# A written order of steps in a cross-covariance attention and MLP kernel: the whole order replaced

## The chip, the cores and the metric

One Trainium2 chip, one of its cores. The metric is the device time of one execution in microseconds (us); lower is better. The kernel before takes 698.52 us (median of 3 runs, 698.0 to 699.55).

## The reference

Inputs are q, k and v of shape (4, 6080, 256), w_in (256, 2048) and w_out (2048, 256), all float32; tau is 1.

```python
qn = q / (np.linalg.norm(q, axis=1, keepdims=True) + 1e-06)
kn = k / (np.linalg.norm(k, axis=1, keepdims=True) + 1e-06)
s = kn.transpose(0, 2, 1) @ qn / tau          # 256 x 256 for each batch
a = softmax(s)                                # along the last axis
x = (v @ a).reshape(24320, 256)
h = x @ w_in
g = 0.5 * h * (1.0 + np.tanh(c * (h + 0.044715 * h * h * h)))
out = g @ w_out
```

## The kernel before

**Algebra.** v @ a @ w_in is computed as v @ aw with aw = a @ w_in, so each batch first needs q^T k (tile G), the sums of squares of q and k, the scores, and then aw (256 x 2048, bf16). The 24320 rows are cut into 48 blocks n, 12 for each batch, of 512 rows (448 in the last block of a batch). A block's work is h = aw^T v^T (2048 x rows), gelu, and w_out^T g. Most of both products is done with seven products of half size in place of eight (the Strassen-Winograd scheme), which needs sums and copies on DVE and ACT around the matmuls.

**The steps.** After a fixed opening (first batch's G and squares, scores, the first quarter of aw), everything is written out by hand as a list of strings, `ORDER`, one string for each block. A step is a name and an offset in blocks: `M3A-2` in block 5's string is step M3A of block 3. `step(what, n)` (L934) turns it into instructions; each engine runs its own instructions in exactly this order, and waits for others through semaphores. The steps:

- `g0`..`g7`: pair p of h done directly (`mm1`, L511, matmul L521, four of 512 columns), into one of two bank pairs "h" and "b" in PSUM; `G0`..`G7`: its gelu on ACT (L531).
- `w0`, `w1`, `w2` with `m1`..`m7`: a set of two pairs done with seven products (`small`, L576, matmul L604, two of 256 columns each); `cq`, `y5` (ACT, L620, L623), `ap`, `ax` (DVE, L625, L628) are copies and sums in between, `Gq`, `Gr`, `Gx` (ACT, L630, L635, L638) the gelus. `cq` has to be through before `m6` and `m2`, `ap` before `m3`, `ax` before `m4`.
- `vs`: sums of v^T for the sets on DVE (L558 to L561); `SW0`..`SW2`: sums of aw (L547 to L550).
- `T1a`, `T2`, `T3`, `T4`: sums of g on DVE (L696 to L711); `M1A`..`M7B`: halves of the seven products with w_out (`product`, L716, matmul L736, four of 256 columns); `y5`, `cq` (ACT, L759, L794), `c11`, `ap`, `ax`, `c12`, `c21`, `c22` (DVE, L765, L774, L798): the combination and the 32 x 32 turning of the result. Four turned pieces start the four stores of a block on SP (L835). `D..`: direct products for the last block (L748), `sA`, `sB` its stores (L823).
- `aw2`..`aw7` (L454) and `ac2`..`ac7` (L465, L467): parts of aw and their scaling; `pA..`, `pF..`, `pS..`, `pNA`: sums and casts of w_out; `vtp`, `vtc`, `vtq`, `vtr`: v of blocks 1 and 2 turned on PE and copied by DVE.
- `row0`..`row5` (`gram_row`, L253), `qsq`, `ksq` (L192, L194), `f1`..`f3`, `sp`, `sa`, `pow`, `kf`, ... : the next batch's G, squares, norms and scores.
- `lq`, `lk` (`load_one`, L98, POOL): a chunk of q or k of the next batch, cast to bf16 on the way; `lv` (L152, POOL): a block of v cast to bf16 into DRAM; `lt` (`load_vt`, L162, SP): that block read back transposed. `lq`, `lk` and `lv` also wait until the last matmul of `mm1` or `small` named ahead of them has run (`GATE`), so their place in the order sets their earliest time.

POOL does little but start loads; SP starts the transposing loads and the stores, in the order of the list. w_in comes in five pieces, columns 0 to 256, to 512, to 1024, to 1536 and to 2048, started in the opening (L905); `aw2` and `aw3` need the third piece, `aw4` and `aw5` the fourth, `aw6` and `aw7` the fifth.

Of the kernel before, what the change touches and what calls it, by code (L numbers as in the profile page):

```python
# [18 lines left out]
def kernel(  # L19
# [1004 lines left out]
    w2Gx row1-1 w1m6 w1ap vs+1 M2B-1 M6B-1 M6A-1 w1m7 qsq row0 M2A-1""",
    """g0 ksq w1m2-1 w1m3-1 w1ax-1 w1m4-1 w1Gr-1 c11-2 ap-2 T4-2 w1Gq-1 w2m4-1 M3A-2 lq+2 M3B-2
    sp-2 T1a-1 sa-2 M7A-2 M7B-2 row3 G0 lq+1 w2Gr-1 ksq-1 w0m5 w0m1 w0cq w0y5 row4 c12-2 g3 G3
    w1Gx-1 w0m6 ax-2 M4B-2 w1m1 M4A-2 vs+1 w1m5 w0ap w0m7 c21-2 w0ax T3-1 w0m2 w0m3 M1B-1 lk+2
    w1y5 row3-2 w0m4 w1cq w1m6 M1A-1 M5A-1 M5B-1 w1ap w1m2 w1m3 T2-1 w0Gq w0Gx w1m7 row2 lk+1
    w0Gr y5-1 cq-1 qsq M2A-1 M6A-1 M6B-1 M2B-1 w1Gq f1-1 w1ax w1m4 w2m1 w1Gr w2m5 f2-1 row0-2""",
    """w0m5 c11-2 w0m1 ap-2 M7B-2 T4-2 w2y5-1 w2cq-1 c22-3 M7A-2 ax-2 w2m6-1 w2ap-1 w0cq row1-1  # L1030
    row0-1 w0m6 w0y5 M4A-2 w0ap M4B-2 w2m7-1 w2m3-1 w2m2-1 M3B-2 w0m2 M3A-2 lk+6 w0m7 T1a-1
    w1Gx-1 w2ax-1 qsq+1 w2Gq-1 c12-2 c21-2 w2Gx-1 w2m4-1 w2Gr-1 g0 G0 M1B-1 f3-2 lt+2 w0m3 w0Gq
    sp-2 w0ax M1A-1 vs+1 sa-2 w0m4 w0Gr g3 M5B-1 G3 M5A-1 w2m5 row1+1 y5-1 cq-1 T3-1 lv+3 lt+3
    c22-2 row5-1 w1m1 w1m5 T2-1 w2m1 T4-1 M6A-1 M6B-1 w0Gx w1cq f1-1 w1y5 w1m6 w1ap M2A-1 M2B-1
    c11-1 ap-1 row5 row0+1 lv+7 w2y5 w2cq row0 w2m6 w2ap qsq w1m7 ksq+1 w1m3 w1m2 w1Gq M7A-1
    w1ax w1Gx M7B-1 M3B-1 w2m7 M3A-1 T1a row2+1 w1m4 w2m3 w1Gr w2m2""",
    """w0m5 row5 ax-2 M4B-2 f2-2 f3-2 w2ax-1 sp-2 sa-2 w2Gq-1 M4A-2 row2-1 w0m1 w0y5 g3 c21-2 c12-2
    c22-2 lv+4 w2Gx-1 T3-1 w2m4-1 T2-1 row4-1 M1A-1 M1B-1 w0cq w0m6 G3 M5A-1 M5B-1 g0 ksq-1 w0ap
    w0m7 f1-1 w0m2 w2Gr-1 f2-1 y5-1 cq-1 G0 w0m3 w0Gq M6B-1 M6A-1 w1m1 w1m5 w1cq w1y5 M2A-1
    row3-1 w0ax M2B-1 w0m4 w0Gr w1m6 T4-1 g4 lt+3 f3-1 sp-1 w0Gx c11-1 ap-1 M7A-1 w1ap w1m7 w1m2  # L1040
    w1m3 G4 w1Gq vs+1 w1ax M7B-1 sa-1 g7""",
    """w0m1 ax-2 f1-1 f2-1 f3-1 M3B-2 w0m5 G7-1 w0cq w0y5 w1m4-1 w1Gr-1 M3A-2 c12-2 lq+4 T1a-1 g0
    w0m6 G0 w0ap M4A-2 row3-4 M4B-2 w1Gx-1 c21-2 w1m1 T2-1 w1m5 w1cq row4-1 w0m7 w0ax w1y5 w0m3
    w0m2 c22-2 lt+3 w0Gq w0Gx M1A-1 w1m6 w1ap M1B-1 M5A-1 T3-1 w0m4 w0Gr M5B-1 row1-2 w1m2 w2m5
    y5-1 sp-1 w1m3 sa-1 w1m7 vs+1 w1ax cq-1 M6B-1 row3-1 w2y5 w2m1 pow w1Gq kf gc M6A-1 T4-1
    M2B-1 M2A-1 g3 c11-1 ap-1 w1m4 kr lq+5 w2cq G3 w2m6 w2ap krp M7B-1 S0+1 lv+4 S1+1 w1Gr w1Gx
    M7A-1 ax-1 c22-1 T1a w2m3 w2m2 w2Gq w2m7 w2ax""",
    """w0m1 w0m5 M3A-2 w0cq M4A-2 lk+4 M4B-2 M3B-2 c12-2 c21-2 th1 w0m6 w0y5 th0 w0ap dn rc2 g0
    M1A-1 M5B-1 w2Gx-1 w0m3 rc0 G0 rc3 w2m4-1 w2Gr-1 w0m2 M1B-1 T2-1 g3 w0Gq G3 lt+3 rc1 M5A-1
    y5-1 g4 cq-1 w0m7 w0ax G4 w1m5 w1m1 M6B-1 M6A-1 M2B-1 w1cq w1y5 T3-1 w0m4 w1m6 M2A-1 w1ap g7  # L1050
    ksq+3 G7 w0Gx w1m7 w1m2 w1m3 c11-1 w1Gq ap-1 M3A-1 eT M3B-1 w0Gr T4-1 rsum+1 rs+1""",
    """g3 G3 M7B-2 vs lt+3 M7A-2 w1ax-1 w1Gx-1 lq+6 c12-2 ax-2 aw0 w0m1 ac0 w0m5 w1m4-1 lq+4 w0cq
    w0y5 g0 vs+1 G0 w0m6 w0ap aw1 ac1 M4A-2 M4B-2 w1m5 w1y5 c21-2 w0m7 aw2 w0ax M1A-1 w0m2 ac2
    w0m4 w0m3 T1a-1 M1B-1 w1Gr-1 w0Gr aw3 ac3""",
    """w0m1 lv+3 w1m1-1 lk+3 w0Gq-1 w1cq-1 M5A-2 M5B-2 g7-1 w1m6-1 aw4-1 T2-2 T3-2 y5-2 cq-2 M2B-2
    w0Gx-1 M6A-2 M6B-2 M2A-2 G7-1 w1ap-1 w1m7-1 qsq+2 w1m2-1 w1m3-1 lk+5 g4-1 SW0-1 ac4-1 c11-2
    ap-2 M7A-2 aw5-1 M7B-2 T4-2 w1Gq-1 T1a-1 G4-1 ac5-1 c22-3 w0m5 w0cq w0y5 M3B-2 M3A-2 c12-2
    w1ax-1 aw6-1 ac6-1 ax-2 w0m6 w1Gx-1 g3 G3 w1m4-1 w1Gr-1 qsq+1 aw7-1 M4B-2 w0ap ac7-1 M4A-2
    c21-2 c22-2 g0 M1A-1 G0 M1B-1 M5B-1 M5A-1 y5-1 w0m7 w1m1 cq-1 SW1-1 T2-1 w1m5 w0m3 w0m2 lk+4
# [12 lines left out]
    w1Gq w1ax ksq+1 w2m6 M7B-1 w1m4 w1Gr row5-1 w2ap w1Gx M7A-1""",
    """w0m5 T1a-1 row2-1 w0m1 M3A-2 w0cq w2m7-1 w2ax-1 w0y5 M3B-2 w0m6 w2Gx-1 ax-2 w2m3-1 w2m2-1
    w2m4-1 w2Gq-1 w2Gr-1 M4A-2 w0ap M4B-2 lt+3 f2-2 w0m7 w0m2 w0m3 w0Gq g3 c21-2 w0ax c12-2 w0m4
    w1m1 M1B-1 f3-2 c22-2 G3 M5A-1 M5B-1 w0Gx w0Gr T2-1 w1m5 w1cq M1A-1 vs+1 w2m5 sp-2 sa-2
# [204 lines left out]
```

## Time and profile before

| | us |
|---|---|
| median of 3 runs | 698.52 |
| the profiled execution's own time | 698.25 |
| its span | 696.5 |
| PE busy | 677.6 |
| DVE busy | 630.3 |
| ACT busy | 625.6 |
| POOL busy | 73.7 |

The span runs from the first to the last instruction; the execution's own time is 1.75 us longer. Matmuls overlap in their records, so the busy time of PE is more than its columns take; the distance between the starts of neighbouring matmuls tells more. Idle time of an engine is listed with what ended it.

### The profile page before, as it was taken

The numbers are of one execution on the slowest core, as the hardware profiler recorded it, in microseconds if no ns is written. First come the engines' busy times: TensorE is split into PE (matmuls) and PEld (weight loads), VectorE is DVE, ScalarE is ACT, GpSimd is POOL, SyncE is SP. The second block draws the span as 40 slices with busy tenths as digits, with TensorE's granted clock in tenths as the row PEclk, the third lists the DMA queues.
The fourth block names the chain that finished last, engine by engine and source line by source line (L and its number), as shares of the span: only waits on it lengthen the run. The fifth ranks groups of instructions, "written<-read, shape, count | busy, mean of one in ns | idle before, by whom it ended". The sixth has DMA issues, their size and how long they took to land.

```text
span 696.5 us, 14682 instructions
## 1 busy us (share of the span) xinstructions
PE 677.6 (97%) x5707; PEld 543.1 (78%) x5707; DVE 630.3 (91%) x1111; ACT 625.6 (90%) x945; POOL 73.7 (11%) x135
## 2 busy tenths in 40 slices
...
PEclk9999999999999999999999999999999999999999
...
GB/s 242 207 268 100 190 142 124 133 128 80 140 129 128 115 69 93 140 160 86 133 105 155 98 90 104 131 100 75 29 106 44 121 78 87 110 52 82 35 75 58
DMA packets 161462, 79.08 MB, mean 114 GB/s; under 512 B 148448, under 2 KB 152160, under 8 KB 160672
## 3 DMA queue, kind: packets, MB, share of 16 engines
...
q8 instruction: 44, 0.72, 0.4%
...
## 4 chain that ended last, share of the span: by engine, by line
PE 78%; ACT 12%; DMA 5%; issue 2%; DVE 1%; ACTq 0%; POOL 0%; SPq 0%; DVEq 0%; POOLq 0%
PE rp L736 35%; PE h L521 14%; PE rb L604 13%; PE qp L604 10%; PE G L253 4%; DMA last<-in_k_dram 2%; ACT g L630 2%; ACT g L531 2%; PE awp L454 2%; ACT sq L192 2%; ACT g L635 1%; ACT qp L620 1%; ACT yw L623 1%; DMA qk_f<-in_q_dram 1%; ACT g L638 1%
## 5 line engine op out<-in xcount | busy, mean ns | idle before, releaser
L736 PEld LDWEIGHTS <-wcomb 128*128 128x128 bf16 x2632 | 255.7, 98 | 45.8 <-issue 2.7
L736 PE MATMUL rp<-t,wcomb 128*128 128x256 bf16 (+1 forms) x1504 | 207.2, 272 | 0.1
L736 PE MATMUL rp<-g,wcomb 128*128 128x256 bf16 (+1 forms) x1128 | 160.7, 272 | 0.0
L531 ACT ACTIVATE g<-h 128x1024 bf16<-128x1024 f32 (+1 forms) x136 | 137.4, 1018 | 14.3 <-PE h L521 13.1
L630 ACT ACTIVATE g<-qp 128x1024 bf16<-128x1024 f32 (+1 forms) x124 | 125.1, 1013 | 7.4 <-PE qp L604 5.4
L521 PE MATMUL h<-vT,aw 128*128 128x512 bf16 (+1 forms) x456 | 115.8, 376 | 0.0
L604 PEld LDWEIGHTS <-sw 128*128 128x128 bf16 x992 | 96.1, 98 | 23.1 <-issue 2.2
L625 DVE TENSOR_TENSOR qp<-rb,yw 128x512 f32<-128x512 f32 (+1 forms) x124 | 85.1, 688 | 9.9 <-PE rb L604 4.9
L604 PE MATMUL rb<-tv,sw 128*128 128x256 bf16 (+1 forms) x496 | 92.6, 271 | 0.2
L628 DVE TENSOR_TENSOR xw<-rb,yw 128x512 f32<-128x512 f32 (+1 forms) x124 | 83.7, 675 | 4.8 <-PE rb L604 2.9
L604 PEld LDWEIGHTS <-aw 128*128 128x128 bf16 x744 | 72.4, 98 | 13.5 <-issue 0.7
L521 PEld LDWEIGHTS <-aw 128*128 128x128 bf16 x544 | 52.7, 98 | 38.5 <-DVE aw L362 0.6
L638 ACT ACTIVATE g<-xw 128x512 bf16<-128x512 f32 (+1 forms) x124 | 77.1, 626 | 1.2 <-DVE xw L628 0.8
L620 ACT ACTIVATE qp<-rb 128x512 f32<-128x512 f32 (+1 forms) x124 | 72.0, 584 | 6.5 <-PE rb L604 2.8
L623 ACT ACTIVATE yw<-qp 128x512 f32<-128x512 f32 (+1 forms) x124 | 73.3, 595 | 4.1 <-PE qp L604 1.9
L635 ACT ACTIVATE g<-rb 128x512 bf16<-128x512 f32 (+1 forms) x124 | 72.7, 594 | 4.4 <-PE rb L604 4.1
L192 ACT ACTIVATE sq<-t 128x1536 bf16<-128x1536 bf16 (+4 forms) x49 | 64.3, 1332 | 7.5 <-DMA t<-in_q_dram 7.5
L774 DVE STREAM_TRANSPOSE ot<-rp 128x256 f32<-128x256 f32 (+1 forms) x141 | 59.2, 434 | 7.0 <-PE rp L736 5.5
L253 PE MATMUL G<-t 128*128 128x256 bf16 (+1 forms) x352 | 58.8, 275 | 1.2 <-DMA t<-in_k_dram 1.2
L707 DVE TENSOR_TENSOR t<-g,t 128x2048 bf16<-128x2048 bf16 (+1 forms) x47 | 56.4, 1201 | 1.0 <-ACT g L638 0.7
L711 DVE TENSOR_TENSOR t<-g,t 128x2048 bf16<-128x2048 bf16 (+1 forms) x47 | 56.7, 1207 | 0.4
L696 DVE TENSOR_TENSOR t<-g 128x2048 bf16<-128x2048 bf16 (+1 forms) x47 | 56.5, 1202 | 0.3 <-ACT g L531 0.2
...
## 6 DMA issues: line engine op xcount, KB each, us to landing
...
```

Of the source, the lines that this page charges most:

```text
L253: nc.tensor.matmul(G[b][:, jc, :], lhsT=qt[:np_, r, jc * 128 : jc * 128 + 128], rhs=kt[:np_, r, :], start=first and jc == 0, stop=jc == 1, ...
L521: mm = nc.tensor.matmul(hp[:, u, :cols], lhsT=AW[b][:, cc, fc * 128 : fc * 128 + 128], rhs=vt_tiles[n][:, cc, :cols], start=cc == 0, stop= ...
L531: nc.scalar.activation(gs(n)[:, 2 * p : 2 * p + 2, :cols], HP.pop((n, p))[:, :, :cols], AF.Gelu_apprx_tanh)
L604: GATE[0] = nc.tensor.matmul(acc[:, u * hc : u * hc + hc], lhsT=lhs[:, u * 128 : u * 128 + 128], rhs=rhs, start=m in (1, 5) and u == 0, st ...
L620: nc.scalar.activation(qp(n, i)[:, 0, :c], RB[n, i][:, :c], AF.Copy)
L623: nc.scalar.activation(YW[n, i][:, :c], qp(n, i)[:, 1, :c], AF.Copy)
L625: nc.vector.tensor_add(qp(n, i)[:, 1, :c], RB[n, i][:, :c], YW[n, i][:, :c])
L628: nc.vector.tensor_add(XW[n, i][:, :c], RB[n, i][:, :c], YW.pop((n, i))[:, :c])
L630: nc.scalar.activation(gs(n)[:, 2 * pa : 2 * pa + 2, :c].rearrange("p u (t x) -> p t u x", t=2), QP.pop((n, i))[:, :, :c].rearrange("p t ( ...
L635: nc.scalar.activation(gs(n)[:, 2 * pb : 2 * pb + 2, :hc], two(RB.pop((n, i))[:, :c]), AF.Gelu_apprx_tanh)
L638: nc.scalar.activation(gs(n)[:, 2 * pb : 2 * pb + 2, hc:c], two(XW.pop((n, i))[:, :c]), AF.Gelu_apprx_tanh)
L736: nc.tensor.matmul(ACCS[n, acc][:, :hc], lhsT=wcomb[:, w, fc, :], rhs=x, start=first and k == 0, stop=k == 3, skip_group_check=True)
```

## The change

Only the 48 strings of `ORDER` change. Every step is there as often as before and every instruction has the same size; what changes is the order of the steps, and with it the order of instructions on each of the five engines' queues and the time at which loads may start. The parts of aw are taken in the order in which their pieces of w_in were started (aw3, aw2, aw4, ...; before aw4, aw2, aw3, ...). Loads of q, k and v are placed so that at most two are meant to be outstanding when another is issued. The rest of the order is written anew around these two points. The first four and the last string:

```diff
-    """g0 lv+3 aw4 ac4 aw2 ac2 aw3 ac3 aw5 ac5 G0 g1 aw6 G1 ac6 lq+1 pS3 g2 G2 g3 G3 pA21 aw7 ac7
-    lk+1 vtp vtc1 vtc0 pA11 g7 vtq vtr1 g6 G7 G6 g5 M1A M1B G5 pA12 lt+3 lv+4 T1a pF0 pS1 g4 G4
-    lq+2 lk+2 lt+4""",
+    """g0 lv+3 aw3 G0 aw2 g1 ac2 ac3 aw4 G1 aw5 lq+1 ac4 g2 ac5 g3 G2 aw6 G3 g4 ac6 SW0 aw7 G4 g5
+    lk+1 ac7 vtp G5 pA11 g6 vtc0 g7 vtc1 G6 T1a vtq G7""",
-    """g3 G3 lv+4 pF1-1 M5A-1 M5B-1 T2-1 y5-1 cq-1 lq+2 g2 G2 g1 G1 M2B-1 g0 vtr0-1 M2A-1 pS2-1
-    T3-1 M6A-1 SW0-1 G0 lk+2 pNA-1 g7 G7 lq+3 c11-1 g6 M6B-1 G6 T4-1 pS4-1""",
+    """g0 vtr0-1 vtr1-1 lt+2 lv+3 G0 g3 G3 M1A-1 g2 lq+1 G2 g1 pF0-1 lk+1 lt+3 pS1-1 G1 pA12-1
+    M1B-1 M5B-1 M5A-1 g6 g7 pF1-1 pS2-1 T3-1 y5-1 cq-1 M2B-1 T2-1 M6A-1 M6B-1 pS4-1 vs+1 M2A-1
+    c11-1 ap-1 row5 G6 G7 pNA-1 g5 pS3-1""",
-    """w0m1 g5-1 G5-1 g4-1 G4-1 ap-2 M3B-2 M7B-2 M7A-2 M3A-2 lk+2 T1a-1 qsq-1 vs ax-2 w0m5 w0cq g5
-    M4A-2 M4B-2 G5 row3-1 T3-1 c21-2 c12-2 w0m6 w0y5 w0ap T2-1 T4-1 g0 G0 M1A-1 M5A-1 w0m2 w0m3
-    w0Gq lt+3 M1B-1 M5B-1 y5-1 cq-1 w0m7 w0ax c22-2 g3 G3 lv+6 g6 G6 w0Gx M6A-1 w0m4 w0Gr M2B-1
-    M6B-1 ksq-1 M2A-1 SW2-2 f1-1 g4 G4 c11-1 g7 G7 ap-1 M3A-1 ksq lv+4 M3B-1 T1a""",
+    """w0m1 g4-1 G5-1 M3B-2 T4-2 G4-1 T1a-1 w0m5 M3A-2 w0cq w0y5 M7A-2 M7B-2 ax-2 lq+1 pA21-2 w0m6
+    w0ap g5 G5 row2-1 T2-1 M4B-2 M4A-2 c21-2 w0m2 w0m3 qsq-1 c12-2 g0 G0 ksq w0Gq lk+1 M1A-1
+    ksq-1 M5A-1 w0m7 M1B-1 lq+2 w0ax w0Gx M5B-1 y5-1 cq-1 g3 g6 G6 w0m4 T3-1 M6A-1 M2A-1 w0Gr
+    T4-1 c22-2 M6B-1 M2B-1 G3 g4 qsq vs+1 lk+2 c11-1 ap-1 lq+3""",
-    """g3 G3 M7B-2 vs M7A-2 w0m5 w0m1 w1m1 ax-2 M4A-2 M4B-2 T3-1 w0cq w0y5 w0m6 w0ap g0 lk+2 c12-2
-    c21-2 c22-2 qsq-1 row1-2 w0m7 w0m2 w0m3 M1B-1 M5A-1 M5B-1 G0 w0ax w0Gq M1A-1 y5-1 cq-1 g7 G7
-    w0m4 T2-1 SW1-3 M6A-1 w1m5 w1cq M6B-1 M2B-1 w1y5 lq+2 w0Gx w0Gr M2A-1 T4-1 w1m6 g4 G4 lv+4
-    f2-2 f3-2 c11-1 ap-1 M7A-1 w1ap qsq+1 M3B-1 w1m7 T1a w1ax M3A-1 M7B-1 ax-1 c12-1 sp-2 sa-2
-    w1m2""",
+    """w0m1 M7B-2 SW1-3 G4-1 M7A-2 M3B-2 M3A-2 f1-2 f2-2 g7-1 G7-1 g3 w1m1 c12-2 ax-2 f3-2 M4A-2
+    row3-1 T1a-1 w0m5 T3-1 M4B-2 c21-2 G3 w0cq w0y5 g0 w0m6 M1A-1 SW2-3 w0ap lv+2 M1B-1 lv+5 G0
+    M5B-1 M5A-1 y5-1 cq-1 w0m2 w0m3 T2-1 c22-2 w1m5 w0m7 w0Gq row2 M6A-1 w1cq M2B-1 g7 G7 w1y5
+    M6B-1 M2A-1 T4-1 w0ax vs+1 w0m4 w1m6 row1+1 g4 w0Gr lt+2 c11-1 ap-1 w0Gx M3A-1 lv+3 G4 M7B-1
+    w1ap lk+2 M3B-1 M7A-1 qsq+1 ksq+1 w1m7""",
...
-    """w0m5 w2m7-1 w0m1 g3 c12-2 c21-2 T1a-1 M1A-1 w0y5 w2ax-1 w0cq w0m6 w0ap w1Gx-1 M1B-1 M5B-1 G3
...
-    w2ap w2m7 w2m3 w2m2 w1ax w1Gx w2Gq c21-1 c22-1 D2a w2ax g0 D6a D5a w2Gx D4a G0 D7a D0a c12
-    c22 sA D5b w1m4 w1Gr D1b w2m4 w2Gr D3b D2b D6b D7b D0b D4b c21 c11 sB""",
+    """w0m5 c21-2 w0y5 w0m1 w0cq g3 M1B-1 w2Gx-1 G3 M1A-1 w0m6 T1a-1 M5A-1 M5B-1 y5-1 cq-1 w1m4-1
...
+    w2Gq w2m7 g0 G0 c21-1 c22-1 D2a w2ax D5a D6a w2Gx D1a D4a D7a D0a c22 c12 w2m4 w2Gr D0b w1m4
+    w1Gr D1b D3b D4b D5b sA D6b D2b D7b c11 c21 sB""",
```

More of the change, by code (lines that the diff above doesn't have):

```diff
@@ L1024 @@
[L1024 to L1059, printed above, removed]
@@ L1072 @@
[L1072 to L1075, printed above, removed]
-    row5-1 f1-1 row5+2 w1m6 w2m1 y5-1 cq-1 M6B-1 M2A-1 M2B-1 w1y5 w1ap w1m7 T4-1 f2-1 w2y5 w2cq
-    w2m6 w2ap qsq w1m3 w1m2 row4+1 row2+1 row1-2 w1Gq M6A-1 w2m3 w2m2 g0 w2m7 f3-1 w1ax w2Gq
@@ L1114 @@
-    y5-1 krp-1 cq-1 M6A-1 M2A-1 w1cq lq+3 M6B-1 w0Gq w1y5 S0 w1m6 th0 S1 th1 M2B-1 dn w0m4 w0Gr
-    g4 G4 T4-1 w1ap w1m7 w1m3 w1m2 w1Gq c11-1 ap-1 M3B-1 rc3 w0Gx M3A-1 M7B-1 rc2 rc0 rc1""",
-    """g3 lk+4 M7A-2 g0-1 G3 ax-2 eT-1 g7-1 M4A-2 G0-1 M4B-2 w0m1 G7-1 w1ax-1 w0m5 w0cq w0y5 T1a-1
-    rsum rs w1m4-1 g0 G0 c12-2 w1Gr-1 c21-2 w0m6 aw0 M1A-1 M5A-1 w0ap w0m7 w1m5 w1Gx-1 ac0 w1m1
-    vs+1 w0ax aw1 M1B-1 M5B-1 w0m3 w0m2 T2-1 lk+5 w1y5 w1cq w1m6 w0m4 w1ap ac1 y5-1 cq-1 w0Gq
-    aw2 ac2 M6A-1 M2A-1 w0Gr w2m5 c22-2 w0Gx w1m7 w2m1 w2y5 w2cq w1ax aw3 ac3 w1m3 M2B-1 c11-1
@@ L1120 @@
-    lt+3 w1Gx w2m6 w1m4 w1m2 w1Gr aw4 w2ap M6B-1 w2m7""",
-    """w0m1 w2m3-1 SW0-1 lk+5 ac4-1 w1Gq-1 w2m2-1 ap-2 T3-2 aw5-1 M3A-2 ac5-1 w0m5 M3B-2 aw6-1
-    M7B-2 w2Gq-1 w0cq M7A-2 w2ax-1 T4-2 ax-2 T1a-1 g3 w2Gx-1 w0m6 M4A-2 w2m4-1 w0y5 w0ap ac6-1
-    G3 aw7-1 ac7-1 M4B-2 qsq+1 lv+3 lv+4 w0m3 w0m2 w0Gq w0m7 g0 G0 lq+4 w2Gr-1 c21-2 c12-2 M1A-1
-    M1B-1 M5B-1 M5A-1 y5-1 cq-1 g7 G7 w1m1 SW1-1 w1m5 M2B-1 T2-1 M6A-1 w1cq w1y5 vs+1 T4-1 M6B-1
-    w0ax w0Gx c22-2 M2A-1 c11-1 w1m6 w1ap w0m4 w0Gr lv+7 lt+3 g4 G4 ap-1 lv+6 w1m3 w1m7 w1m2
@@ L1175 @@
-    """w0m5 w0y5 w0m1 w0cq g3 ax-2 c22-2 M4B-2 w1ax-1 rc0 G3 w1Gx-1 w0m6 w0ap w1m4-1 w1Gr-1 M4A-2
-    g7-1 G7-1 w0m2 w0m3 w0Gq c12-2 c21-2 M1A-1 M5A-1 M5B-1 y5-1 g0 G0 rc1 rc3 eT w0m7 w0ax M1B-1
-    rsum+1 cq-1 g4 w0Gx w0m4 w0Gr lv+3 w1m5 T2-1 w1m1 w1cq G4 rs+1 M2B-1 T4-1 w1y5 vs+1 M2A-1
-    aw0+1 M6A-1 ac0+1 w1m6 lv+4 w1ap M6B-1 g7 G7 c11-1 aw1+1 ap-1 ac1+1 T3-1 w1m7 w1ax w1m3 w1m2
-    M3B-1 M3A-1 c12-1 aw2+1 ac2+1 w1Gq lt+3 w1Gx""",
-    """g0 M7B-2 G0 w0m5 T1a-1 w0m1 M7A-2 aw3 ax-2 w0cq w0m6 ac3 w0y5 w0ap g3 G3 w1m4-1 w1Gr-1 SW0
```

398 lines of the change are left out of this document (230 added, 168 removed).

## Prediction

> **What bounds the kernel now.** I read the page first, then the chain of waits, the groups by form, the timeline of the stretches around each edit, and the landing times of loads.
>
> ```profile
> span 696.5 us, 14682 instructions
> PE 677.6 (97%) x5707; PEld 543.1 (78%) x5707; DVE 630.3 (91%) x1111; ACT 625.6 (90%) x945; POOL 73.7 (11%) x135
> PEclk9999999999999999999999999999999999999999
> ```
> PE is the bound, at a full granted clock; DVE and ACT have about a tenth of slack. A busy PE need not be a PE at its pace, so the pace comes from the chain:
>
> ```profile
> 31.80 7.66 DMA win_bf<-in_moe_w_in_dram
> 39.50 1.89 PE awp L454 x8
> 58.59 1.73 PE h L521 x8
> 70.10 1.31 PE rp L736 x12
> 690.27 1.76 PE o L748 x16
> ```
> Twelve 256-column matmuls take 1.31 us, 109 ns each; eight 512-column ones take 1.73 us, 216 ns each. How many there are is in the groups by form (a weight load stands for its matmul):
>
> ```profile
> L736 PEld LDWEIGHTS <-wcomb 128*128 128x128 bf16 x2632 | 255.7, 98 | 45.8 <-issue 2.7 <-DVE ot L774 1.4 <-DVE t L707 0.4
> L604 PEld LDWEIGHTS <-sw 128*128 128x128 bf16 x992 | 96.1, 98 | 23.1 <-issue 2.2
> L253 PE MATMUL G<-t 128*128 128x256 bf16 x344 | 57.4, 275 | 1.2 <-DMA t<-in_k_dram 1.2
> L604 PEld LDWEIGHTS <-aw 128*128 128x128 bf16 x744 | 72.4, 98 | 13.5 <-issue 0.7
> L521 PEld LDWEIGHTS <-aw 128*128 128x128 bf16 x544 | 52.7, 98 | 38.5 <-DVE aw L362 0.6 <-DVE aw L467 0.5 <-issue 0.2
> L748 PEld LDWEIGHTS <-wcomb 128*128 128x128 bf16 x64 | 6.1, 98 | 0.9 <-issue 0.5
> L454 PEld LDWEIGHTS <-eT 128*128 128x128 bf16 x60 | 5.8, 98 | 2.7 <-issue 1.0
> ```
> (2632 + 992 + 744) x 0.109 = 476; (544 + 60) x 0.216 = 130.5; of the G matmuls 62 belong to the opening, 282 x 0.109 = 31; 64 D matmuls of 224 columns x 0.096 = 6. That is 643.5 us; the narrower last blocks take off some 5 us and the small matmuls add as much. From the first h matmul (37.74, shown below) to the end of the last o matmul (690.27 + 1.76 = 692.03) pass 654.3 us. So **all waiting of PE under the written order is about 11 us**, and a new order, which changes no work and starts at 37.74 as before, can only move these 11 us. Of them 1.35 lie in the first eight microseconds and 0.5 in the tail (below); the other 9 are spread in pieces of at most 0.3 us.
>
> **The head: aw parts and the first g steps.**
>
> ```profile
> 37.74 1.04 PE L521 MATMUL h<-vT_pe,aw 128*128 128x512 bf16 x4 [0.36 <-DVE aw L362]
> 38.97 1.02 ACT L531 ACTIVATE g<-h 128x1024 bf16<-128x1024 f32 x1
> 39.50 1.89 PE L454 MATMUL awp<-win_bf,eT 128*128 128x512 bf16 x8 [0.72 <-DMA win_bf<-in_moe_w_in_dram]
> 40.13 3.38 DVE L467 TENSOR_SCALAR aw<-awp,rs 128x512 bf16<-128x512 f32 x5 [1.66 <-PE awp L454]
> 44.68 0.61 PE L323 MATMUL vt_ps<-ident_bf,v 128*128 128x128 bf16 x8
> 45.57 1.02 PE L521 MATMUL h<-vT_pe,aw 128*128 128x512 bf16 x4 [0.29 <-ACT g L531]
> 30.25 0.70 POOL L905 DMA_DIRECT2D win_bf<-in_moe_w_in_dram  x1 [0.61 <-DMA last<-in_q_dram]
> DMA to landing us min/median/max: 7.5/7.6/8.9
> ```
> The last line is for the five pieces of w_in. g0 ends its issue at 37.74 + 4 x 0.216 = 38.60; aw4 needs the fourth piece, issued 31.80, landing 39.46: PE waits 0.9. The vtp transposes are through at 45.12 (8 x 0.055), g7 starts at 45.57: 0.45 more, for a bank that G still reads. Sum 1.35.
> After the change aw3 and aw2 follow g0; their piece, issued 30.25, lands by 30.25 + 7.5 = 37.8: no wait. Then by hand: aw3 38.60, aw2 39.03, g1 39.47, aw4 40.33 (its piece is there at 39.46), aw5, g2 41.20 (ac2 and ac3 at 0.68 each from 39.66 are done at 41.0). The g steps alternate between two bank pairs, each 0.86 of PE work, then 0.37 until ACT starts, then 1.0 of G. Carried on so to block 2, this gives waits of 0.15 (g4), 0.1 and 0.1 (g2, g1 of block 1), 0.25 (M2B of block 0: pA12 stands ahead of y5 and cq on ACT) and 0.1 (g5): 0.7. **Gain 0.65**, between 0 (if ACT is later than my count) and 1.35.
>
> **The loads.** POOL issues each load when the last g or set matmul named before it has run, so its place in the order sets its time. I count places as PE work from the first g0. The change moves the loads of batch 1 later and closer to their use: q3 from place 13 to 23, k4 from 23 to 33, the v of block 5 from 12 to 40. The work that covered them is gone from between. The tightest is k of block 2 (chunk 1): issued at place 14.4, after g1 of block 1, at 53.4; its square stands on DVE in block 2. DVE's queue up to it, from 39.66, by these rows,
>
> ```profile
> 45.55 0.74 DVE L329 COPY vT_pe<-vt_ps 128x512 bf16<-128x512 bf16 x2
> 47.42 1.22 DVE L696 TENSOR_TENSOR t<-g 128x2048 bf16<-128x2048 bf16 x1
> 48.70 1.23 DVE L668 TENSOR_TENSOR wf<-wst,wst 128x1024 f32<-128x1024 f32 x1
> 49.97 0.69 DVE L670 CAST wcomb<-wf 128x1024 bf16<-128x1024 f32 x1
> ```
> is six ac (4.1), SW0 (1.0), pA11, pS1, pS2 (2.0), pF0, pF1, pS4, pS3 (4.8), four vt copies (1.5), six T sums (7.0) and some 3.5 of smaller ones, 24 us, with 2.2 us of waits for PE: it reaches the square at 65.8. So this load has 12.4 us. What loads took at that time and later, and transposes of v on SP beside them:
>
> ```profile
> 51.35 0.54 POOL L98 DMA_DIRECT2D t<-in_k_dram  x1
> DMA to landing us min/median/max: 17.7/17.7/17.7
> DMA to landing us min/median/max: 4.2/4.7/9.0
> DMA to landing us min/median/max: 27.6/27.6/27.6
> DMA to landing us min/median/max: 2.9/3.9/8.5
> 55.00:60.00 5.00, 5.00 (x32) 2.96 (x31) 4.72 (x10) 4.48 (x6) 1.05 (x2) 1.00 2.31 41
> 72.34 0.95 DVE L194 TENSOR_TENSOR sq<-t 128x1536 bf16<-128x1536 bf16 x1
> ```
> In order: this same k load in the trace of before (issued 51.35) and its landing time; q and k loads after 130 us; the transpose of block 4, issued at 54.8; transposes after 130 us; the stretch 55 to 60, in which all DMA moved 41 GB/s; and the same square, which ran at 72.34, after the landing at 69.1. So the change asks for this square 6.5 us earlier and issues its load 2 us later. With 4.7 to 12.4 us to landing it costs nothing; with 17.7 it lands at 71.1 and DVE stands 5.3 us; PE first waits for w0ax behind it, and the DVE steps up to ap (block 1) have 0.9 us in hand, so PE loses 4.4. The slow stretch comes when the transposes of blocks 3 and 4 meet q and k loads; eight loads of q, k and v stand at places 10 to 23 before, three after the change. I take 0 as likeliest, since most of the crowd is gone, and keep 4.4. The transpose of block 5 has 10.7 us to its use where it had 28.7: its cost lies in the same bracket. All other leads are 9.6 us or more (transposes near the end 5.4), above the 4.7 and 3.9 of the rows after 130.
> The Trainium skill ("DMA: Bandwidth & Descriptors", Queues, rings and completion order) says that a DMA engine takes turns between its queues packet by packet. The trace agrees as far as 27.6 against 3.9 us for one kind of transpose goes; by that rule fewer loads outstanding let transposes land sooner, and the sum stays at a cost of 0.
>
> **The middle.** What is left of waiting there comes from short ways between PE, ACT and PE:
>
> ```profile
> 321.83 1.03 PE L521 MATMUL h<-vT,aw 128*128 128x512 bf16 x4
> 322.29 0.58 ACT L620 ACTIVATE qp<-rb 128x512 f32<-128x512 f32 x1
> 322.93 0.38 PE L604 MATMUL rb<-tv,sw 128*128 128x256 bf16 x2
> ```
> The h matmuls are issued by 322.69; the m6 matmuls start at 322.93, after the copy cq on ACT (to 322.87): 0.24 lost. Counting PE work between m1 and m6 in both orders, 29 of 124 places have under 1.3 us before, 21 after; from M4 and M3 to the next M1, 17 of 46 have under 1.1 us before, 11 after; from one use of a g bank pair to the next, 59 of 258 have under 1.53, then 45. The shortfalls under 1.32 of these three sum to 14.2 us before and 8.8 after; other kinds hardly differ. ACT and DVE work in the heaviest 20 us of PE work is 26.5 and 26.2 us by mean durations before, 26.8 and 25.4 after: no new heap. If all 9 us went with the shortfalls, 3.3 would go; if these counts say nothing, none, and an order can also be worse by as much. I take a third: **gain 1.0**, range -3.3 to +3.
>
> **The tail.**
>
> ```profile
> 688.77 0.85 ACTq L823 DMA_DIRECT2D out_dram<-ot  x2
> 688.98 0.93 PE L748 MATMUL o<-g,wcomb 128*128 128x224 bf16 x8
> 689.67 0.98 ACT L635 ACTIVATE g<-rb 128x448 bf16<-128x448 f32 x2 [2.28 <-PE rb L604]
> ```
> The two stores of sA stand on ACT ahead of both Gr; these start at 689.67, when the stores are issued, and PE, through at 688.98 + 8 x 0.096 = 689.75, waits until 690.27. In the new order both Gr stand before sA and five D steps between: the wait goes, and the last transposes and stores follow 0.5 earlier. **Gain 0.5** (0 to 0.5).
>
> **Sum.** 0.65 + 1.0 + 0.5 = 2.15. The profiled execution took 698.25, the median of the runs is 0.27 above: 698.25 - 2.15 = 696.1, so 696.4 as a median.
>
> **Rivals.** (1) The loads are late: all as above, but the k load takes 17.7 us as it did. 698.25 - 2.15 + 4.4 = 700.5, as a median 700.8: slower. It decides from a landing 17 us after issue on; for it speaks the row itself, against it the three loads instead of eight in that stretch. The Trainium skill (same page, Rules for kernel authors) asks to issue a DMA early and wait late, which the change does less; the cover of this load goes from 23.1 to 12.4 us of PE work, and what that costs by the rule is this rival's price. (2) Half late: landing at about 68.5, when the slow stretch ends as before (69.1 less half a load), costs 1.8: 698.25 - 2.15 + 1.8 = 697.9, as a median 698.2, no change. (3) The middle turns out worse by 3: 698.25 - 1.15 + 3 = 700.1, 700.4 as a median. (4) The pacing is not what happens, since the order fixes places and not landings; if v, q, k and two transposes overlap anyway this is (1) or (2).
>
> **Numbers.** Forecast 0.44, (1) 0.2, (2) 0.2, (3) 0.16; (4) is in these. The measurement tells 0.2%, 1.4 us, from no change. Forecast and the good side of the middle give faster 0.42; (2) and the weak edge of the forecast give 0.24 for the same; (1) and (3) leave 0.34. The range goes from 694.0 (the middle at -3.3) to 701.5 (rival 1 with the transpose of block 5 adding to it); the forecast's own range is 694.0 to 697.5.
>
> **What would show it.** Right: awp starts at 38.6 with no DMA ahead of it, no DVE or PE wait on a landing of q, k or vT after 40 us, Gr before ACT's stores, fewer m6 gaps. Wrong: DVE idle ahead of a square at line 194 near 66, or ahead of the v sums at line 558 near 97; then PE loses what DVE stood beyond 0.9 us.

## The result, and the profile after

| | us |
|---|---|
| after, median of 8 runs | 696.70 (696.63 to 696.96) |
| before, median of 8 runs beside it | 699.03 (698.0 to 702.2) |
| ratio after / before, 95% interval | 0.996 (0.9942 to 0.9978) |
| the profiled execution after, and its span | 696.96, 695.2 |

The forecast was 696.4, and faster. The order before does not take one time: of 130 executions of it in this study 72 took 697.9 to 699.0 (their median is 698.22), 15 took 699 to 701 and 43 more than that. Where a ratio is given, executions over 1.5% above the quickest are left out of it, which is one of the 130. So the change has two gains: 1.5 us against the quick executions of before (1.29 between the two profiled spans), and the rest because none of its 8 runs is a long one.

The page after, to be set beside the two lines of before:

```profile
span 695.2 us, 14706 instructions
PE 677.7 (97%) x5707; PEld 543.8 (78%) x5707; DVE 630.0 (91%) x1111; ACT 624.0 (90%) x945; POOL 74.5 (11%) x135
```

Busy times of PE, DVE and ACT are the same to 0.3%: work didn't change, only waiting. The head, in the timeline (start, duration, engine, line, tiles, count, and in brackets the idle time ahead with what ended it):

```profile
37.85 1.04 PE L521 MATMUL h<-vT_pe,aw 128*128 128x512 bf16 x4 [0.37 <-DVE aw L362]
38.73 1.03 PE L454 MATMUL awp<-win_bf,eT 128*128 128x512 bf16 x4
39.59 1.03 PE L521 MATMUL h<-vT_pe,aw 128*128 128x512 bf16 x4
40.46 1.03 PE L454 MATMUL awp<-win_bf,eT 128*128 128x512 bf16 x4
41.32 1.89 PE L521 MATMUL h<-vT_pe,aw 128*128 128x512 bf16 x8
45.64 0.61 PE L323 MATMUL vt_ps<-ident_bf,v 128*128 128x128 bf16 x8
46.08 1.89 PE L521 MATMUL h<-vT_pe,aw 128*128 128x512 bf16 x8
```

From 37.85 on each row starts where the one before it runs out: 4 x 0.216 gives 38.71, and so on (the rows between 43.05 and 45.64 are left out and do the same). There is no bracket with a DMA, and none ahead of the h matmuls at 46.08 where before had 0.29 at 45.57.

The loads that the prediction weighed: the transposes of blocks 3 and 4 (issued 49.9 and 54.9), q and k loads issued between 50 and 56 (the second is k of block 2, 52.64, landing 60.39), the stretch 55 to 60 (busy time of each engine, granted clock of PE, DMA share, GB/s), and the square that needs this k:

```profile
DMA to landing us min/median/max: 6.0/6.2/6.4
DMA to landing us min/median/max: 6.2/7.0/7.8
55.00:60.00 5.00, 5.00 (x39) 3.62 (x38) 4.83 (x9) 4.54 (x6) 0.00 (x0) 1.00 1.16 197
64.30 1.79 DVE L194 TENSOR_TENSOR sq<-t 128x1536 bf16<-128x1536 bf16 x2
```

16 to 27.6 us have become 6.0 to 6.4, 17.7 has become 7.8, 41 GB/s 197, and the square starts at 64.30 without a wait, 8 us earlier than before. The tail:

```profile
687.51 1.12 ACT L635 ACTIVATE g<-rb 128x448 bf16<-128x448 f32 x2 [1.49 <-PE rb L604]
687.89 2.85 PE L748 MATMUL o<-g,wcomb 128*128 128x224 bf16 x28
688.15 4.24 ACTq L823 DMA_DIRECT2D out_dram<-ot  x4
```

Gr stands ahead of ACT's stores, and the last 28 direct matmuls run in one piece.

**Where the time went, stretch by stretch.** Matmul columns are fixed, so one can count PE's work from the first g0 on (109 ns for 256 columns): a matmul's place. The time at which it starts less its place is PE's lag; where it rises, PE waited. From the matmul records of the two traces:

| place | lag before | lag after | after less before |
|---|---|---|---|
| 0 | 37.74 | 37.85 | +0.11 |
| 2 | 38.62 | 37.85 | -0.77 |
| 30 | 39.04 | 37.79 | -1.25 |
| 100 | 40.06 | 38.39 | -1.67 |
| 300 | 42.40 | 40.99 | -1.41 |
| 600 | 45.66 | 45.19 | -0.47 |
| 640 | 46.01 | 45.41 | -0.60 |
| end of the last matmul (us) | 692.01 | 690.73 | -1.28 |

The lags rise by less than PE waits, because the 108 one-column matmuls, whose starts lie 25 ns apart, are counted wider than that; the differences between the two columns change by about 0.1 us with it. Added up from neighbour to neighbour, PE's gaps are 10.6 us before, where the prediction had 11, and 9.2 after.

Head: -1.25, or -1.36 from the +0.11 at which the order starts. Tail, from 640 on: -0.68. The middle, where I had expected 1.0 more, gave back 0.65, all of it and more between places 100 and 600.

### The profile page after: what moved, and what is told of

It reads as the page before. It is cut to its first block, busy times and chain, and to the rows that moved or that the text cites. A ratio compares the mean times of both kernels' runs of the same rounds, so it can differ in the third digit from the quotient of the medians.

```text
span 695.2 us, 14706 instructions
## 1 busy us (share of the span) xinstructions
PE 677.7 (97%) x5707; PEld 543.8 (78%) x5707; DVE 630.0 (91%) x1111; ACT 624.0 (90%) x945; POOL 74.5 (11%) x135
## 3 DMA queue, kind: packets, MB, share of 16 engines
q10 hardware_dynamic: 1248, 1.28, 0.6%
## 4 chain that ended last, share of the span: by engine, by line
PE 82%; ACT 8%; DVE 4%; DMA 4%; issue 1%; DVEq 0%; POOL 0%; ACTq 0%; POOLq 0%
PE rp L736 36%; PE h L521 15%; PE rb L604 13%; PE qp L604 10%; PE G L253 4%; DMA t<-in_k_dram 3%; PE awp L454 1%; DMA t<-in_q_dram 1%; ACT g L531 1%; ACT yw L623 1%; ACT qp L620 1%; ACT g L635 1%; ACT sq L192 1%; PE o L748 1%; ACT g L630 1%
## 5 line engine op out<-in xcount | busy, mean ns | idle before, releaser
L736 PE MATMUL rp<-t,wcomb 128*128 128x256 bf16 (+1 forms) x1504 | 209.3, 272 | 0.1
L531 ACT ACTIVATE g<-h 128x1024 bf16<-128x1024 f32 (+1 forms) x136 | 137.6, 1017 | 11.6 <-PE h L521 11.0
L253 PE MATMUL G<-t 128*128 128x256 bf16 (+1 forms) x352 | 60.6, 277 | 0.6 <-DMA t<-in_k_dram 0.6
```

What stands on the lines that cost most here:

```text
L253: nc.tensor.matmul(G[b][:, jc, :], lhsT=qt[:np_, r, jc * 128 : jc * 128 + 128], rhs=kt[:np_, r, :], start=first and jc == 0, stop=jc == 1, ...
L531: nc.scalar.activation(gs(n)[:, 2 * p : 2 * p + 2, :cols], HP.pop((n, p))[:, :, :cols], AF.Gelu_apprx_tanh)
L736: nc.tensor.matmul(ACCS[n, acc][:, :hc], lhsT=wcomb[:, w, fc, :], rhs=x, start=first and k == 0, stop=k == 3, skip_group_check=True)
```

## The experiments

In diffs the steps are written as in the order; "..." stands for steps that stay. Each was timed in turn with before on the same chip: E0 to E3 together, then E4 to E7, E8 to E10, and E11. After was not timed again beside them; the quick executions of before, which were, have medians of 698.19 to 698.31 in all the groups, so a difference to after is good to about 0.1 us. Where two traces have the same order of g steps, the starts of their gelus (L531) are compared one by one, which shows where two kernels part.

**E0: before, unchanged.** 

> The kernel before, unchanged, as a control. Its eight executions so far lie between 698.0 and 702.2 us, those of the new order between 696.63 and 696.96. Theory 1 (the gain is waiting of PE that the new order takes away in the head and the tail): the profile shows again 37.7 to 692.0 us for the ordered part, and the spread of the old order is a matter of its own. Theory 2 (the gain comes from the loads: transposes and loads in a crowd land late in some executions of the old order): the spread of 4 us is seen again, and a profile of a slow execution has DVE or PE standing at a landing.

698.34 (698.11 to 703.09). Nine of its twelve runs took 698.1 to 698.8, two took 703; beside them the 35 runs of before had a median of 700.4 and went to 708.53. By luck its profile is of one of the long executions (703.02). It matches the profile of before, gelu by gelu, up to 74 us (0.21 earlier throughout), and is 4.05 later at 75 and 4.74 later at 79; it stays so to the end. What happened there; the first two lines are the landing times of the transposes of blocks 3 and 4 and of the q and k loads issued from 50 to 56:

```profile
DMA to landing us min/median/max: 27.0/29.2/31.5
DMA to landing us min/median/max: 20.2/23.4/24.9
55.00:60.00 5.00, 4.95 (x31) 2.94 (x31) 4.96 (x10) 4.49 (x5) 1.05 (x2) 1.00 1.29 27
73.88 0.96 DVE L194 TENSOR_TENSOR sq<-t 128x1536 bf16<-128x1536 bf16 x1 [1.63 <-DMA t<-in_k_dram]
77.03 1.89 PE L521 MATMUL h<-vT,aw 128*128 128x512 bf16 x4 [3.21 <-DMA vT<-vb]
78.71 1.78 PE L736 MATMUL rp<-t,wcomb 128*128 128x256 bf16 x8
80.33 0.38 PE L604 MATMUL qp<-tv,sw 128*128 128x256 bf16 x2
75.00:80.00 5.00, 2.97 (x11) 1.50 (x12) 1.98 (x4) 1.02 (x1) 0.00 (x0) 0.68 1.09 174
```

For comparison, the landing time of the same transpose in the profile of before, issued at 49.8, and the matmuls that use it first:

```profile
DMA to landing us min/median/max: 16.0/16.0/16.0
73.85 1.03 PE L521 MATMUL h<-vT,aw 128*128 128x512 bf16 x4
```

The transposed v of block 3, issued 49.98, lands at 76.98 and not at 66 as in the profile of before, where it had 8 us to spare; all DMA moves 27 GB/s where it moved 41. PE stands 3.2 us for it. Then the four h matmuls take 1.68 us up to the next row, 0.42 each in place of 0.216, and the eight of 256 columns behind them 1.62 us, 0.20 each in place of 0.109: half the pace, and a granted clock of 0.68 over the stretch. Of the 4.95 us lost here, 0.82 + 0.75 = 1.6 are due to the clock and 3.4 to standing. The Trainium skill ("TensorE: Matmul & The Clock Gate", Part 1: The HAM clock gate) says that the clock falls to half after an idle window of about 3.4 us, and rises again after as long a busy one. The trace agrees with the half, though the stand was 3.2 us, and with a return within 3.3 us (77.03 to 80.33); E1's trace takes longer to return. So in the one long execution with a trace it is theory 2: PE stands at a landing. Whether the gain over the quick executions comes from the loads, too, is for E2.

**E1: before, the aw parts in the order in which their pieces land, nothing else.**

```diff
-g0 lv+3 aw4 ac4 aw2 ac2 aw3 ac3 aw5 ac5 ...
+g0 lv+3 aw2 ac2 aw3 ac3 aw4 ac4 aw5 ac5 ...
```

> The order before, with aw2, aw3 ahead of aw4, aw5 in the first string; nothing else moved. Theory 1: the wait of 0.9 us for the fourth piece of w_in goes, the wait of 0.45 us for a bank at 45 us stays: 697.1 to 697.6 us, and the ordered part of the profile is 0.9 us shorter. Theory 2: no change.

702.71 (701.82 to 705.12), ratio to before 1.0031 (1.0002 to 1.006).

```profile
38.43 2.08 PE L454 MATMUL awp<-win_bf,eT 128*128 128x512 bf16 x8
44.58 0.62 PE L323 MATMUL vt_ps<-ident_bf,v 128*128 128x128 bf16 x8 [0.62 <-DMA v<-in_v_dram]
77.51 1.89 PE L521 MATMUL h<-vT,aw 128*128 128x512 bf16 x4 [3.81 <-DMA vT<-vb]
75.00:80.00 5.00, 2.49 (x8) 1.19 (x9) 1.68 (x4) 0.56 (x1) 0.00 (x0) 0.60 1.13 174
80.00:85.00 5.00, 5.00 (x31) 3.54 (x29) 2.67 (x5) 3.33 (x5) 0.06 (x1) 0.71 1.14 189
```

The wait for the fourth piece of w_in is gone (gelus 0.69 earlier at 42 us), but 0.58 of that is given back by 48 us: PE, being earlier, waits for v of block 1, whose load hasn't moved. Then this kernel shows the late landing of E0: counted from the gelus at 48 us, they are 4.8 us later at 75 and 6.6 later at 82. All ten runs are long (701.82 and more); that they all land late is inferred from that, as only one has a trace. The clock costs more than in E0: after a stand of 3.8 us the granted clock is below 1 in the stretch 80 to 85 as well. A mean of 0.71 over 5 us means (1 - 0.71) x 5 / 0.5 = 2.9 us at half, so PE works at half from 77.51 to about 82.9 and loses some 2.7 us (an estimate from these rows). Neither expectation came true: an edit that is right by itself was worth 0.1 us here, and set off a loss of 6.6 us elsewhere. That the loss is made by the loads and not by the aw parts is what E7 tests.

**E2: before, with the loads and transposes of the first 100 us at the places that they have after.** All other steps stay in the old order.

```diff
-... lq+1 pS3 ... lk+1 vtp ... lt+3 lv+4 T1a pF0 pS1 g4 G4 lq+2 lk+2 lt+4
-g3 G3 lv+4 ... lq+2 ... lk+2 ... lq+3 ...
+lv+3 at place 0.9, lq+1 3.5, lk+1 7.8, lt+3 and lv+4 11.3, lq+2 13.5, lk+2 and lt+4 14.4,
+then q of block 3 at 23.3, k at 26.8, q and k of block 4 at 28.3 and 33.3, v of block 5 at 40.0, ...
```

> The order before, with the loads of q, k, v and the transposes of the first 100 us of PE work at the places of the new order; all other steps stay. Theory 1: the time stays at that of the fastest executions before, 698.0 to 698.5 us, since no PE or DVE wait on a load stands in the profile of before after 40 us; the k load of block 2 lands in under 9 us in place of 17.7, the transpose of block 4 in under 8 in place of 27.6. Theory 2: the time falls to 696.7 to 697.2 us and its spread to under 0.5 us.

698.29 (697.84 to 698.73), ratio 0.9966 (0.994 to 0.9991). First the landing of the transposes of blocks 3 and 4, then the stretch in which E0 lost its time:

```profile
DMA to landing us min/median/max: 6.1/6.1/6.2
75.00:80.00 5.00, 5.00 (x44) 4.01 (x42) 4.31 (x10) 4.62 (x6) 0.48 (x1) 1.00 0.89 163
```

All twelve runs lie within 0.9 us, at the level of the quick runs of before. The pacing gains nothing over those, since their transposes came in time, as theory 1 had it; it takes away the long executions, which is all that it does. The gelus of this kernel are those of before to 0.07 us from end to end.

**E3: after, with the early loads crowded again.**

```diff
 lv+4, lq+2, lk+2, lv+5, lq+3, lk+3, lq+4, lk+4 (first batch's blocks): back at the old places,
-11.3, 13.5, 14.4, 40.0, 23.3, 26.8, 28.3, 33.3
+10.4, 11.3, 11.3, 12.2, 13.1, 17.0, 17.8, 22.8
```

> The new order, with eight loads (v of blocks 4 and 5, q and k of chunks 1 to 3 of batch 1) moved ahead to their old places; all else stays. Theory 1: 696.7 us, within 0.3; loads land in 15 to 20 us again and the transposes of blocks 3 and 4 in 16 to 28, but all before their use. Theory 2: 698 to 702 us with a spread of some us.

696.86 (696.57 to 697.37), 0.16 above after. Transposes of blocks 3 and 4 in this trace, who waited for them, and the stretch 55 to 60:

```profile
  DVE tv L558: 0.6, 1
DMA to landing us min/median/max: 15.5/17.6/19.7
55.00:60.00 5.00, 4.95 (x39) 3.71 (x39) 4.83 (x9) 4.54 (x6) 1.12 (x3) 1.00 1.10 192
```

The crowd makes the transposes late again, by 9 to 14 us. In the profiled execution (the slowest of the twelve, 697.37) that costs 0.15 by 68 us and 0.58 more by 74; over all runs a fifth of that. The k load of block 2 landed 10.3 us after its issue. So in the new order the pacing of these loads is a safeguard worth 0.2 us; in the old one, pacing was worth the whole spread. But this is not the trouble of E0: all DMA moves 192 GB/s in the stretch where it moved 27 and 41 there, and none of the twelve runs is long. So these eight loads alone do not bring the slow stretch back. E2 moved the transposes along with the loads, while here the transposes keep their new places; which of the two keeps the stretch away is not shown.

**E4: both orders mixed.** The new order's strings 0 to 18, then what is left in the old order up to string 43, then the rest in the new.

> The new order's strings 0 to 18, then what is left of the steps in the old order up to string 43, then what is left in the new order. Theory (the middle of the new order waits more than the old one did): between places 300 and 600 the lag of PE behind its own work rises by 42.40 to 45.66 = 3.26 us in the old order and by 40.99 to 45.19 = 4.20 in the new, so this mixture keeps head and tail of the new order and gains 0.7 to 1.0 on it: 695.7 to 696.0, below both kernels. Rival (the rise is not a matter of these strings; it comes from the work itself, or the seams cost as much as they save): 696.5 to 697.5.

696.32 (696.17 to 696.70), ratio 0.9951 (0.9927 to 0.9974): the fastest kernel of the study, 0.4 under after, less than expected. Between places 300 and 600 its lag rises by 44.78 - 41.42 = 3.36 us, that of before by 3.26, that of after by 4.20: the old order waits 0.9 less there, so the loss of the middle is a matter of its order. The seam takes half of it: between 250 and 300 the mixture's lag rises by 1.64, that of after by 1.14.

**E5: after, aw4 first again.**

```diff
-g0 lv+3 aw3 G0 aw2 g1 ac2 ac3 aw4 G1 aw5 lq+1 ac4 g2 ...
+g0 lv+3 aw4 aw3 G0 aw2 g1 ac4 ac2 ac3 G1 aw5 lq+1 g2 ...
```

> The new order with aw4 ahead of aw3 and aw2, as it was, and nothing else moved. Theory (the head's gain is the wait for the fourth piece of w_in): PE stands about 0.8 us ahead of aw4 (38.7 to 39.5) and keeps that: 697.4 to 697.6. Rival (PE would be held up a little later all the same, by g and its banks or by v, so the wait is taken from slack): 696.7 to 697.0.

697.61 (697.42 to 698.39), 0.91 above after. As the theory said:

```profile
39.19 1.46 PE L454 MATMUL awp<-win_bf,eT 128*128 128x512 bf16 x6 [0.76 <-DMA win_bf<-in_moe_w_in_dram]
```

Its gelus are 0.45 earlier than those of after at 39 us and 0.63 later at 42 (1.08 lost in this execution, whose opening ended early), and 0.74 later at the end. Nothing behind the head gives it back.

**E6: after, sA's stores ahead of Gr again.**

```diff
-... c22 c12 w2m4 w2Gr D0b w1m4 w1Gr D1b D3b D4b D5b sA D6b ...
+... c22 c12 sA w2m4 w2Gr D0b w1m4 w1Gr D1b D3b D4b D5b D6b ...
```

> The new order with the two stores of sA on ACT's queue ahead of both Gr again. Theory (the tail's gain is this place of sA): Gr starts about 0.9 us late, PE stands 0.5 us ahead of the last D steps: 697.2, between 697.0 and 697.5. Rival (five D steps between Gr and its use are cover enough): 696.7.

697.37 (697.18 to 698.32), 0.67 above after; the gelus up to 685 us are those of after (0.05 earlier at the end), the span is 0.54 longer.

```profile
687.83 1.70 PE L748 MATMUL o<-g,wcomb 128*128 128x224 bf16 x16
688.02 0.88 ACTq L823 DMA_DIRECT2D out_dram<-ot  x2
688.94 0.98 ACT L635 ACTIVATE g<-rb 128x448 bf16<-128x448 f32 x2 [2.97 <-PE rb L604]
689.97 1.31 PE L748 MATMUL o<-g,wcomb 128*128 128x224 bf16 x12 [0.44 <-ACT g L635]
```

The wait of before is back: the matmuls issued from 687.83 on are through at 687.83 + 16 x 0.096 = 689.37, and the next start at 689.97.

**E7: before, with E2's pacing, E1's aw order and sA behind Gr.**

> The old order with three local edits: the loads and transposes of the first 100 us at the new places (which alone took 698.29), aw2 and aw3 ahead of aw4 and aw5 (which alone took 702.71, always with the late transpose of block 3), and sA behind w2Gr and five D steps. Theory (late landing of block 3 came from the crowd of loads, not from the order of aw): no PE wait of 3 us or more near 77 us and a granted clock of 1.0 there; 698.3 less 0.2 to 0.9 for aw (v of block 1 lands at 44.5 and limits it) less 0.5 for the tail: 697.0 to 697.6. Rival (the earlier start after the aw change itself makes loads collide): 701 to 703.

697.76 (697.54 to 698.27), ratio 0.9969 (0.9944 to 0.9994). No wait near 77 us: the gelus keep their distance from before to 0.1 us from 48 us to the end. So what E1 lost goes with the old places of the loads and transposes. The head keeps 0.4: 0.88 earlier at 42, 0.44 of it given back by 48, for v again:

```profile
44.38 0.62 PE L323 MATMUL vt_ps<-ident_bf,v 128*128 128x128 bf16 x8 [0.31 <-DMA v<-in_v_dram]
```

Of the tail's 0.5 the span keeps 0.1. PE ends 0.96 us earlier than before, but the last store is issued at 692.93, where after issues it at 692.02; three of SP's four stores only start from 692.07 on. By the semaphores of its trace the first of these waits for the landing of ACT's first store (issued 688.85, landing 692.05); in after that place in SP's queue starts at 688.42, without a wait. What in the order makes this difference wasn't pursued. Three local edits so give a third of what the new order gives against the level of 698.2; 0.8 us of its head, where vtp comes two g steps later, and most of its tail are missing.

**E8, E9, E10: cq ahead of y5.** The search for the middle's loss. In the timeline of after, m6 often waits for cq while ACT runs y5; at 615.84 M2A of the products waits for its cq behind a gelu:

```profile
313.48 0.64 ACT L623 ACTIVATE yw<-qp 128x512 f32<-128x512 f32 x1
313.68 1.02 PE L521 MATMUL h<-vT,aw 128*128 128x512 bf16 x4
314.15 0.58 ACT L620 ACTIVATE qp<-rb 128x512 f32<-128x512 f32 x1
314.79 0.38 PE L604 MATMUL rb<-tv,sw 128*128 128x256 bf16 x2
614.09 1.02 ACT L630 ACTIVATE g<-qp 128x1024 bf16<-128x1024 f32 x1
615.42 0.37 ACT L794 ACTIVATE rp<-rp 128x256 f32<-128x256 f32 x1
615.84 0.93 PE L736 MATMUL rp<-g,wcomb 128*128 128x256 bf16 x7 [0.19 <-ACT rp L794]
```

The h matmuls end their issue at 313.68 + 4 x 0.216 = 314.55; m6 starts at 314.79, when cq is through. Adding up all such gaps over 0.06 us between places 8 and 632: m6 1.59 us before, 2.55 after; M2A 0.16 and 1.10. In 68 of the 124 sets y5 stands ahead of cq, in both orders, and there lie 1.59 and 2.26 us of m6's waits. So in three kernels (after, E4, E2) y5 was put right behind cq in those 68 sets:

```diff
-... w0m5 w0y5 ... w0m1 w0cq ...
+... w0m5 ... w0m1 w0cq w0y5 ...
```

> The new order with y5 put right behind cq in the 68 sets where it stood ahead of it (the sets' steps alone; in the products y5 has to be first). In the profile of after PE waited 2.55 us at m6 between places 8 and 632, 2.26 of them at 14 of these 68 places and 0.29 at 3 of the other 56. Theory (what the middle gives back is cq standing behind y5 on ACT, 0.6 us each): most of the 2.26 goes: 694.5 to 695.5. Rival (ap then waits for y5 and m3 for ap, or the same wait comes back at M2 and M6): 696.3 to 697.0.

> The mixture of both orders (new head, old middle, new tail; 696.32 us) with the same move of y5 behind cq in its 68 places, where PE waited 2.30 us at m6. Theory: 694.1 to 695.1, the fastest so far. Rival: 696.0 to 696.6.

> The old order with paced loads (698.29 us) and the same move of y5 behind cq in its 68 places, where the old order waited 1.59 us at m6 at 9 places. Theory: 696.7 to 697.6, and less gain than in the new order. Rival: 698.0 to 698.6.

701.56 (701.2 to 703.27), 702.99 (702.7 to 706.3) and 704.46 (704.38 to 705.13): 4.9, 6.7 and 6.2 us slower than what they were made from. The theory fell, by its sign, in all three. The groups of cq, after and then E8 (busy, mean ns, idle ahead of it with what ended it):

```profile
L620 ACT ACTIVATE qp<-rb 128x512 f32<-128x512 f32 (+1 forms) x124 | 71.9, 583 | 8.3 <-PE rb L604 2.9 <-PE qp L604 2.6
```

```profile
L620 ACT ACTIVATE qp<-rb 128x512 f32<-128x512 f32 (+1 forms) x124 | 72.7, 587 | 14.3 <-PE rb L604 10.9 <-PE qp L604 2.3
```

m6's own waits did fall (to 0.67 us, by a trace in which 66 matmul records are missing), but ACT now stands 6.0 us more for m1, time in which y5 used to run. The time grew by 4.9 us, not at one point but in steps of 0.1 to 1 us from 108 us on. In the matmul records PE's waits, after and then E8, are 0.43 and 2.44 us at m5, 1.10 and 1.96 at M2A, 0.75 and 1.29 at M6B and 0.22 and 0.85 at m1, most of them ended by ACT; m3, which the rival named, has none over 0.06. So ACT's standing comes back at PE almost in full. "About a tenth of slack" on ACT isn't slack at these places. One of the twelve runs of E8 (703.27) and one of E9 (706.30) is long although their loads are paced; neither has a trace, and why is open.

**E11: cq ahead of y5 in seven sets only,** those where m1 was through before y5 began (sets 0, 1, 1, 1, 2, 1 and 0 of blocks 8, 16, 28, 35, 29, 43 and 20).

> The new order with y5 put behind cq in seven sets only: those where, in the profile of after, m6 waited and the last matmul of m1 had ended 0.08 us or more before y5 began, so that ACT could have run cq at that moment; together 1.40 us of waits at m6. Moving it in all 68 sets cost 4.9 us, with ACT standing ahead of cq 14.3 us in place of 8.3. Theory (cq first helps where m1 is through, and costs where ACT has to stand for it): 695.3 to 696.3. Rival (whatever is taken from m6 turns up at the next wait, as ACT has no slack there): 696.5 to 697.0. That y5 is wanted early for its own sake: over 697.

696.44 (696.05 to 696.60), ratio 0.9959 (0.994 to 0.9978), 0.26 under after: between the two theories. The set at 314 us again:

```profile
312.95 0.64 ACT L620 ACTIVATE qp<-rb 128x512 f32<-128x512 f32 x1
313.15 1.02 PE L521 MATMUL h<-vT,aw 128*128 128x512 bf16 x4
314.01 0.38 PE L604 MATMUL rb<-tv,sw 128*128 128x256 bf16 x2
```

m6 follows h 0.86 later (4 x 0.216) in place of 1.11, and so in all seven sets: 1.40 us of waits at m6 are gone. Comparing gelu by gelu with after, the distance is -0.54 up to 316 us (the opening ended earlier in this execution), and grows by 0.16 at 320, 0.07 at 439, 0.06 at 535 and 0.06 at 635: 0.37 of the 1.40 stays. The other three sets leave nothing. In the matmul records 0.17 us is back at m6 of the next set in blocks 35 and 43, and 0.10 at m4 of the same set in block 29: a wait taken from m6 mostly turns up soon behind it.

## Why the prediction was right, and where it was not

It said 696.4 and faster; 696.70 was measured. Its terms, against the two profiles:

| term | forecast | profiles | by experiment |
|---|---|---|---|
| start of the order | 0 | +0.11 | the opening's doing |
| head (to place 30) | -0.65 | -1.36 | E5: 0.91 of it is aw4's place |
| loads | 0 | 0 | E3: eight loads back cost 0.16 |
| middle | -1.0 | +0.65 | E4: 0.9 more waiting than the old order has |
| tail (from place 640) | -0.5 | -0.68 | E6: 0.67 |
| sum | -2.15 | -1.28 | |

The sum is 0.87 too large. The median comes within 0.3 all the same because the profiled execution of after lies 0.26 above its median, while I had set the median 0.27 above the profile, as for before. That closeness is luck, and so is that two terms were off with opposite signs.

*The head* was under-sized. Both waits that I found (0.9 and 0.45) were real and both went; the 0.7 of new waits that I counted by hand did not come. The step that failed is "then 0.37 until ACT starts":

```profile
37.78 1.28 ACT L916 ACT_TABLE_LOAD   x1
39.08 1.02 ACT L531 ACTIVATE g<-h 128x1024 bf16<-128x1024 f32 x1
40.66 1.02 ACT L531 ACTIVATE g<-h 128x1024 bf16<-128x1024 f32 x1 [0.56 <-PE h L521]
42.38 1.94 ACT L531 ACTIVATE g<-h 128x1024 bf16<-128x1024 f32 x2 [0.70 <-PE h L521]
```

I took it from the first gelu (38.97 after h at 37.74), and that one waits for ACT's table load. The others start 1.07 after their h matmul, 0.2 after its last issue (39.59 to 40.66, 41.32 to 42.38). A bank pair is so ready after 0.86 + 0.2 + 1.0 = 2.06 us, and g4 comes 2.16 after g2.

*The loads* came out as forecast: 7.8 us for the load that had 12.4, no wait on a landing after 40 us, and rivals (1) and (2) with them not true. The reading that "the slow stretch comes when the transposes of blocks 3 and 4 meet q and k loads" was too simple: in E3 they meet, the transposes are late, and there is no slow stretch. What I missed is which order was in danger. I read the row with 41 GB/s as a price that the old order had paid already; it was eating a margin. With the transpose of block 3 landing 16 us after its issue PE lost nothing and had 8 us left; with 27 us, in E0's profile, it lost 4.95, and 43 of 130 executions were 2.8 us or more above the level of 698.2 (that one is the only one of them with a trace). One profile shows one landing.
The Trainium skill ("DMA: Bandwidth & Descriptors", Queues, rings and completion order), by which a DMA engine takes turns between its queues, agrees with E2 and E3: the same transposes take 6.1 us without and 15.5 to 19.7 with the crowd of loads. It doesn't account for the 27 GB/s of E0's stretch, where E3's crowd moved 192.

*The middle* had the wrong sign. The step that failed is the count of short ways: shortfalls between m1 and m6 fell from 29 places to 21, while places with a wait at m6 rose from 9 to 17 (1.59 us before, 2.55 after); "fewer m6 gaps" was one of my signs of being right. PE work between two steps doesn't decide, but what ACT has in front of the copy when its input is there: y5, or a gelu. E8 and E11 show that this isn't cured by moving that copy forward either. I had kept a range of -3.3 to +3 for this term, and rival (3) at 3; 0.65 lies well inside.

*The tail* is right in kind, and 0.2 larger than the 0.5 that I took for its most.

Open: which of the new order's choices makes its middle wait 0.9 us more. E11 takes 0.3 to 0.4 us away, over the whole middle. Between places 300 and 600, where the loss lies, the waits are 0.92 us at m6 and none at M2A before, 1.31 and 0.89 after, 1.04 and 0.26 in E4. So M2A, which waits for its cq on ACT, is the larger part, and E8 to E11 worked on the smaller; single steps of M2A weren't tried.
